# A reordered ramp with dummy matmuls, a last batch gated by token tiles, and out chunks in column tiles: an attention and gated-MLP kernel on one core

## Chip, cores, metric

One core of one Trainium2 chip. The metric is the device time of one execution in microseconds (us), lower is better. An execution takes about 1.8 us more (1.7 to 3.0 in single runs) than its span in the trace, from the first to the last instruction. A run is called fast unless it is over 1.5% above the fastest of the same kernel on that occasion. One of the findings below is that the kernel before has two groups of runs *within* the fast ones, so the text says each time which group it compares.

## The reference

Eight batches. Each is a grouped-query attention (16 query heads, 4 key/value heads, 384 tokens, head size 64), followed by a gated MLP whose gate mixes tokens.

```python
scores = scale * np.matmul(q, k.transpose(0, 1, 3, 2))     # k, v repeated for 4 query heads
attn = np.exp(scores - max); attn = attn / (sum + 1e-09)
x = concat_heads(np.matmul(attn, v))                       # (8, 384, 1024)
h = np.maximum(x @ w_in, 0.0)                              # (8, 384, 1024)
u, v = h[..., :512], h[..., 512:]
v_n = (v - mean(v)) / np.sqrt(var(v) + 1e-06)
v_s = np.einsum('ts,bsd->btd', w_spatial, v_n) + b_spatial[None, :, None]
return ((u * v_s) @ w_out).astype(np.float32)              # (8, 384, 1024)
```

## The kernel before

The whole program is a text of steps, played in order. Each word names a function: `s` a pair of score matmuls, `e` their exp on ScalarE (ACT), `a` an add of two exp tiles on VectorE (DVE), `m` the row sums, `r` the reciprocal, `x` the value matmuls, `n` the normalisation to xT, `V` and `U` the two halves of the w_in product, `S` the statistics, `rs` the rstd, `vn` v_n, `p` the spatial product, `O` an out chunk of 512 columns, `l..` loads, `c..` casts to half precision, `K`, `Q`, `t..` transposes, `A`, `H` half products of V and U. A quote mark means the batch before, a plus the batch after. So a steady round works on three batches at once.

```python
def play(b, text):
    for word in text.split():
        ...                       # letters: the step; digits: its arguments; ' and +: the batch
            STEPS[op](at, *nums)

def pe_group(dst, pairs):
    n = len(pairs)
    for i, (w, m) in enumerate(pairs):
        nc.tensor.matmul(dst, w, m, start=(i == 0), stop=(i == n - 1))

def project(b, i, split=1):       # O: gT (128x128 weights) times w_out16, 4 matmuls of 512 columns
    ...
    pe_group(banks[:, x, :], [(gT[:, m, tt*P:(tt+1)*P], w_out16[:, m, half*512:(half+1)*512]) for m in range(NDT)])
    nc.vector.tensor_copy(osb[:, half * 512 : (half + 1) * 512], banks[:, x, :])
    ...                           # split == 2: a write of 256 KB for each half

RAMP = "lkg0 lqd00 lqd01 lv lkg1 lqd10 lqd11"
RAMP1 = """
    ckv0 cqv000 cqp001 Ka0 Qj00 Qja01 wv0 cqv010 cqv011
    s0 e0 s1 e1 s2 e2 Q01 ckv1 cqv100 cqv101 s3 e3 K1 s4 e4 Q10 cqv110 cqv111 s5 e5 Q11
    cv wu0 lk+ lq0+ lq1+ lv+ ws ck+ cq0+ wv1
    s6 e6 s7 m00 r00 x000 n000 x001 n001 e7 s8 e8 s9 e9 s10
    ...
    m11 r11 x110 n110 x111 n111 Q10+ Q11+ cws tws"""
C1 = "m10' m11' r10' r11' x100' n100' x101' n101' x110' n110' x111' n111'"
C0 = "m00 m01 r00 r01 x000 n000 x001 n001 x010 n010 x011 n011"
VISITS = [
    "s0 s1 s2 e0 e1 e2 a12' O0'' O1'' lk+ lq0+ lv+ lq1+", C1,
    "s3 s4 s5 e3 e4 e5 V0' S0' V1' S1' a00 a01 ck+ cq0+",
    "s6 s7 s8 e6 e7 e8 V2' S2' O2'' O3'' tk+ tq0+ cq1+ cv+",
    "s9 s10 s11 e9 e10 e11 a02 O4'' rs' O5'' vn' tq1+", C0,
    "s12 s13 s14 e12 e13 e14 p0' U0' p1' U1' a10",
    "s15 s16 s17 e15 e16 e17 p2' U2' p3' U3' a11",
]
...
LAST = """
    a12' O0'' O1'' m10' m11' r10' r11' x100' n100' x101' n101' x110' n110' x111' n111'
    V0' S0' V1' S1' O2'' V2' S2' O3'' rs' vn' O4'' O5''
    p0' p1' U0' p2' U1' p3' U2' U3' O0' O1' O2' O3' Oh4' Oh5'"""

play(0, RAMP); ...; play(0, RAMP1); play(1, FIRST)
for b in range(2, B):
    play(b, STEADY if b > 2 else ...)
play(B, LAST)
```

The softmax here doesn't subtract the row's maximum and nothing guards it: scores larger than these inputs give would overflow.

Of the kernel before, what the change touches and what calls it, by code (L numbers as in the profile page):

```python
# [10 lines left out]
FP32 = mybir.dt.float32  # L11
FP16 = mybir.dt.float16
# [5 lines left out]
def kernel(  # L18
# [11 lines left out]
    nc = tc.nc  # L30
# [53 lines left out]
    def touch(*xs):  # L84
        mark(False, xs)

    def take1():
        x = min((i for i in range(8) if not busy[i]), key=lambda i: used[i])
        mark(True, (x,))
        return x  # L90

    def take2():
# [4 lines left out]
        mark(True, (x, x + 1))  # L97
        return x, x + 1

    def f32(x, n):  # L100
        return banks[:, x, 0:n]

    def f16(x, n):
        return banks[:, x, :].bitcast(FP16)[:, 0:n]

    def pe_group(dst, pairs):
        n = len(pairs)
        for i, (w, m) in enumerate(pairs):
            nc.tensor.matmul(dst, w, m, start=(i == 0), stop=(i == n - 1))  # L109


    ident = cst.tile([P, P], FP32, name="ident")
    ident16 = cst.tile([P, P], FP16, name="ident16")
    ones32 = cst.tile([P, 32], FP16, name="ones32")
    eps_t = cst.tile([P, 1], FP32, name="eps_t")
    bias_raw = cst.tile([P, S], FP32, name="bias_raw")
# [69 lines left out]
    def cast_v(b, engine):  # L186
        engine(T["v16", b].rearrange("p g t d -> p g (t d)"), T["v32", b])

    def load_q(b, gp, qds=(0, 1)):
        if ("q32", b, gp) not in T:  # L190
            T["q32", b, gp] = ld.tile([P, 2, G, NST * D], FP32, name=f"q32_{b}_{gp}", tag=f"q32_{gp}")
            T["q16", b, gp] = qk16.tile([P, G, NST, 2, D], FP16, name=f"q16_{b}_{gp}", tag=f"q16_{gp}")
        heads = q[b, gp * 2 * G : (gp + 1) * 2 * G].rearrange(
            "(a qd) (p t) d -> qd p a (t d)", qd=2, t=NST
        )
        for qd in qds:
            nc.sync.dma_start(T["q32", b, gp][:, qd, :, :], heads[qd])

    def cast_q(b, gp, engine, half, qd):
        engine(  # L200
            T["q16", b, gp][:, 2 * qd : 2 * qd + 2, :, half, :],
            T["q32", b, gp][:, qd, 2 * half : 2 * half + 2, :].rearrange(
                "p j (t d) -> p j t d", t=NST
            ),
        )
# [36 lines left out]
    def turn_q_pe(b, gp, js, copy):  # L242
# [14 lines left out]
        )  # L257
        touch(x)


    def score(b, u):
        gp, c, t = u // 9, (u % 9) // 3, u % 3
# [36 lines left out]
    def add(b, gp, c):  # L299
# [3 lines left out]
        cs = slice(c * 512, (c + 1) * 512)  # L303
        nc.vector.tensor_tensor(T["sT", b, gp][:, :, cs], aT[:, 0, :, cs], aT[:, 1, :, cs], ALU.add)  # L304

    def sums(b, gp, quad):
        x = take1()
        aT, sT = T["aT", b, gp], T.get(("sT", b, gp))
        parts = [aT[:, t] for t in range(NST)] if sT is None else [sT, aT[:, 2]]
        tiles(f32(x, S), quad, [(ones32, a) for a in parts])  # L310
        T["sum", b, gp, quad] = x

    def recip(b, gp, quad):
# [4 lines left out]
        nc.scalar.activation(rec, rec, AF.Exp, scale=-1.0)  # L318
        T["rec", b, gp, quad] = rec

    def value(b, gp, quad, jj):
        v16, aT = T["v16", b], T["aT", b, gp]
        x = take1()
        tiles(
            f32(x, S),
            quad,
            [
                (v16[:, 2 * gp : 2 * gp + 2, t, 32 * jj : 32 * (jj + 1)], aT[:, t])
                for t in range(NST)
            ],  # L330
        )
        T["X", b, gp, quad, jj] = x
# [24 lines left out]
        )  # L357
        return x

    def v_half(b, st):  # L360
        x = v_mm(b, st, range(4))
        if ("vparts", b) not in T:
            T["vparts", b] = ff.tile([P, NST, DH], FP32, name=f"vparts_{b}", tag="part")
        part = T["vparts", b][:, st, :]
        nc.vector.tensor_copy(part, banks[:, x, :])
        touch(x)
        T["vpart", b, st] = part

    def u_half(b, mu):
        x = u_mm(b, mu, range(4))  # L370
        if ("uparts", b) not in T:
            T["uparts", b] = ff.tile([P, NDT, S], FP32, name=f"uparts_{b}", tag="part")
        part = T["uparts", b][:, mu, :]
        nc.vector.tensor_copy(part, f32(x, S))
        touch(x)
        T["upart", b, mu] = part

# [64 lines left out]
        )  # L442
        touch(x)

    def project(b, i, split=1):
        tt, half = i // 2, i % 2
        if half == 0:
            T["osb", b, tt] = outp.tile([P, DM], FP32, name=f"osb_{b}_{tt}", tag="osb")
        osb = T["osb", b, tt]
        gT = T["gT", b]  # L450
        x = take1()
        pe_group(
            banks[:, x, :],
            [
                (gT[:, m, tt * P : (tt + 1) * P], w_out16[:, m, half * 512 : (half + 1) * 512])
                for m in range(NDT)
            ],
        )
        nc.vector.tensor_copy(osb[:, half * 512 : (half + 1) * 512], banks[:, x, :])  # L459
        touch(x)  # L460
        dst = out[b].rearrange("(p t) d -> p t d", t=NST)[:, tt, :]
        if split == 2:
            nc.sync.dma_start(
                dst[:, half * 512 : (half + 1) * 512], osb[:, half * 512 : (half + 1) * 512]
            )
        elif half == 1:
            nc.sync.dma_start(dst, osb)

    vec, act, pool = nc.vector.tensor_copy, nc.scalar.copy, nc.gpsimd.tensor_copy




    STEPS = {
        "s": score, "e": expo, "m": sums, "a": add, "r": recip, "x": value, "n": norm,
        "V": gate_v, "S": stats, "rs": rstd, "vn": lambda b: v_norm(b, nc.vector),
        "p": spatial, "U": gate_u, "O": project, "A": v_half, "H": u_half,
        "lk": load_k, "lq": load_q, "lv": load_v,
        "lkg": lambda b, gp: load_k(b, (gp,)),
        "lqd": lambda b, gp, qd: load_q(b, gp, (qd,)),  # L480
        "ck": lambda b: cast_k(b, pool), "cv": lambda b: cast_v(b, pool),
        "ckv": lambda b, gp: cast_k(b, vec, (gp,)),
        "cq": lambda b, gp: [cast_q(b, gp, pool, half, qd) for qd in range(2) for half in range(2)],
# [4 lines left out]
        "K": lambda b, gp: turn_k_pe(b, gp, vec),  # L488
        "Ka": lambda b, gp: turn_k_pe(b, gp, act),
        "Q": lambda b, gp, i: turn_q_pe(b, gp, (2 * i, 2 * i + 1), vec),  # L490
        "Qj": lambda b, gp, j: turn_q_pe(b, gp, (j,), vec),
        "Qja": lambda b, gp, j: turn_q_pe(b, gp, (j,), act),
        "wv": lambda b, gp: load_w_in(gp, DH, DFF), "wu": lambda b, gp: load_w_in(gp, 0, DH),
        "wo": lambda b: load_w_out(), "ws": lambda b: load_ws(),
        "cws": lambda b: cast_ws(nc.gpsimd), "tws": lambda b: turn_ws(),
        "Oh": lambda b, i: project(b, i, 2),
    }

    def play(b, text):
        for word in text.split():  # L500
            kind = word.rstrip("'+")
            at = b - word.count("'") + word.count("+")
            op = kind.rstrip("0123456789")
            nums = kind[len(op):]
            if 0 <= at < B:
                STEPS[op](at, *([int(nums)] if op in ("s", "e") else map(int, nums)))

    RAMP = """
        lkg0 lqd00 lqd01 lv lkg1 lqd10 lqd11"""
    RAMP1 = """  # L510
        ckv0 cqv000 cqp001 Ka0 Qj00 Qja01 wv0 cqv010 cqv011
        s0 e0 s1 e1 s2 e2 Q01 ckv1 cqv100 cqv101 s3 e3 K1 s4 e4 Q10 cqv110 cqv111 s5 e5 Q11
        cv wu0 lk+ lq0+ lq1+ lv+ ws ck+ cq0+ wv1
        s6 e6 s7 m00 r00 x000 n000 x001 n001 e7 s8 e8 s9 e9 s10
        m01 r01 x010 n010 x011 n011 e10 A0 s11 e11 A1 s12 e12 A2 s13 e13 H0 s14 e14
        K0+ K1+ s15 e15 Q00+ m10 r10 x100 n100 x101 n101 cq1+ wu1 cv+ wo
        s16 e16 Q01+ s17 e17 H1 s0+ e0+ H2 s1+ e1+ H3 s2+ e2+
        m11 r11 x110 n110 x111 n111 Q10+ Q11+ cws tws"""
    C1 = "m10' m11' r10' r11' x100' n100' x101' n101' x110' n110' x111' n111'"
    C0 = "m00 m01 r00 r01 x000 n000 x001 n001 x010 n010 x011 n011"  # L520
    VISITS = [
        "s0 s1 s2 e0 e1 e2 a12' O0'' O1'' lk+ lq0+ lv+ lq1+", C1,
        "s3 s4 s5 e3 e4 e5 V0' S0' V1' S1' a00 a01 ck+ cq0+",
        "s6 s7 s8 e6 e7 e8 V2' S2' O2'' O3'' tk+ tq0+ cq1+ cv+",
        "s9 s10 s11 e9 e10 e11 a02 O4'' rs' O5'' vn' tq1+", C0,
        "s12 s13 s14 e12 e13 e14 p0' U0' p1' U1' a10",
        "s15 s16 s17 e15 e16 e17 p2' U2' p3' U3' a11",
    ]
    STEADY = " ".join(VISITS)
    FIRST = " ".join(w for w in STEADY.replace(C1, "").split() if w not in ("s0", "s1", "s2", "e0", "e1", "e2", "a12'", "a00", "a01", "a02", "a10", "a11"))  # L530
    LAST = """
        a12' O0'' O1'' m10' m11' r10' r11' x100' n100' x101' n101' x110' n110' x111' n111'
        V0' S0' V1' S1' O2'' V2' S2' O3'' rs' vn' O4'' O5''
        p0' p1' U0' p2' U1' p3' U2' U3' O0' O1' O2' O3' Oh4' Oh5'"""

    with tc.manual_schedule():
        play(0, RAMP)
        make_identity(nc, ident)
        nc.vector.tensor_copy(ident16, ident)
        nc.vector.memset(ones32, 1.0)  # L540
        nc.vector.memset(eps_t, eps_ln)
        play(0, RAMP1)
        play(1, FIRST)
        for b in range(2, B):
            play(b, STEADY if b > 2 else " ".join(w for w in STEADY.split() if w != "a12'"))
        play(B, LAST)
# [1 line left out]
_INS = ['q', 'k', 'v', 'moe_w_in', 'moe_w_spatial', 'moe_b_spatial', 'moe_w_out']  # L548
# [26 lines left out]
```

## Time and profile before

| kernel before | |
|---|---|
| time, median of 3 runs | 263.55 us (262.69 to 263.74) |
| span of the profiled run | 260.4 us (that run took 262.19) |
| TensorE (PE) busy | 242.8 us, 93% of the span |
| DVE, ACT, Pool busy | 186.5, 172.6, 58.4 us |
| second value steps of batch 1 begin | 58.89 us |
| last batch's second value steps begin | 232.00 us |

The last two rows cut the span in three: a ramp (58.89 us), a steady middle of twelve half rounds (173.11 us) and a tail (28.42 us). "Value steps" are always the 48 matmuls aT,v of 384 columns, which PE does in one go twice in a batch (the steps C0 and C1 of the text). They are a mark that a trace of either kernel has. Where only a batch is named below, its second ones, C1, are meant. Note that the profiled run took 262.19 us and the three timed ones 262.69 to 263.74: the trace shows one of the quicker runs. That will matter.

### The profile page before, as it was taken

The page shows a single profiled execution, that of the slowest core. Times are in us where ns is not written, and L with a number is a line of the kernel's source. Part 1 is how long each engine was busy: PE and PEld are TensorE (multiplying, and loading weights), DVE is VectorE, ACT ScalarE, POOL GpSimd, SP SyncE. Part 2 cuts the span into 40 slices and gives each one's busy share as a digit, 9 for nine tenths or more (in the row PEclk, how much of TensorE's full clock was granted, in tenths as well). Part 3 has the DMA queues.
Part 4 walks back from the last instruction along what each step waited for, and adds up shares of the span by engine and source line. Part 5 has one row for each costly group of instructions (what it writes and reads, how often), then busy time and mean ns, then how long its engine had stood idle before and what let it go on. Part 6 is the DMA issues. An engine that isn't in the chain of part 4 may idle for free.

```text
span 260.4 us, 5301 instructions
## 1 busy us (share of the span) xinstructions
PE 242.8 (93%) x2140; PEld 110.8 (43%) x2140; DVE 186.5 (72%) x345; ACT 172.6 (66%) x227; POOL 58.4 (22%) x100
## 2 busy tenths in 40 slices
PE   2798998799999999999999999999899999999993
PEld 1333443344355444444354434543354434554451
DVE  2434658885986779766986689676986689587954
ACT  2877989787685877676785868776775858730000
POOL 3639704400720045001800054002600000000000
PEclk9999999999999999999999999999999999999999
DMA  7999999807694299609692398709592204010306
GB/s 213 258 302 303 171 197 317 136 0 242 205 211 104 92 303 184 182 4 277 190 241 51 117 326 136 181 27 280 174 237 45 83 0 164 0 64 20 161 1 242
DMA packets 56920, 41.92 MB, mean 161 GB/s; under 512 B 26304, under 2 KB 53056, under 8 KB 56896
## 3 DMA queue, kind: packets, MB, share of 16 engines
q1 hardware_dynamic: 54048, 38.44, 54.7%
q0 software_dynamic: 2848, 3.15, 7.4%
q8 instruction: 16, 0.26, 0.4%
q14 instruction: 8, 0.07, 0.1%
HBM read 25.95 MB, written 12.58 MB: 148 GB/s over the span
## 4 chain that ended last, share of the span: by engine, by line
PE 67%; DVE 18%; DMA 4%; ACT 4%; issue 3%; SPq 2%; POOL 0%; DVEq 0%
PE banks L109 46%; PE banks L269 10%; PE banks L291 9%; DMA q<-in_q_dram 4%; DVE xT L338 4%; DVE v_n L407 3%; DVE osb L459 3%; ACT aT L281 3%; PE banks L250 2%; DVE sT L304 2%; DVE bn L396 1%; DVE v_r L383 1%; DVE vs L427 1%; DVE uparts L438 1%; SPq L170 1%
## 5 line engine op out<-in xcount | busy, mean ns | idle before, releaser
L281 ACT ACTIVATE aT<-banks 128x1024 f16<-128x1024 f32 x144 | 137.7, 1024 | 50.1 <-PE banks L269 50.0
L269 PE MATMUL banks<-qT,kT 64*128 64x512 f16 x288 | 46.7, 393 | 5.7 <-DVE osb L459 2.0
L109 PE MATMUL banks<-xT,w_in 128*128 128x384 f16 x256 | 47.4, 326 | 0.0
L109 PE MATMUL banks<-w_out,gT 128*128 128x512 f16 x192 | 45.7, 380 | 0.1
L109 PE MATMUL banks<-w_in,xT 128*128 128x512 f16 x192 | 45.1, 380 | 0.7 <-DVE xT L338 0.6
L338 DVE TENSOR_TENSOR xT<-banks,rec 128x384 f16<-128x384 f32 x64 | 31.4, 549 | 14.3 <-ACT rec L318 12.3
L200 POOL CAST q<-q 128x384 f16<-128x384 f32 x57 | 31.8, 587 | 16.3 <-DMA q<-in_q_dram 12.7
L459 DVE COPY osb<-banks 128x512 f32<-128x512 f32 x48 | 32.1, 685 | 4.5 <-PE banks L109 4.2
L291 PE MATMUL banks<-aT,v 128*32 128x384 f16 x768 | 35.3, 332 | 0.0
L109 PEld LDWEIGHTS <-w_in 128*128 128x128 f16 x256 | 24.7, 98 | 17.0 <-issue 0.9
L176 POOL CAST k<-k 128x768 f16<-128x768 f32 x7 | 5.8, 830 | 111.6 <-DMA k<-in_k_dram 111.6
L109 PEld LDWEIGHTS <-gT 128*128 128x128 f16 x192 | 17.5, 98 | 29.8 <-issue 9.3
L440 DVE SCALAR_TENSOR_TENSOR gT<-banks,vs 128x384 f16<-128x384 f32 x28 | 15.6, 557 | 19.3 <-PE banks L109 19.2
L109 PEld LDWEIGHTS <-xT 128*128 128x128 f16 x192 | 17.4, 98 | 26.5 <-issue 6.8
L304 DVE TENSOR_TENSOR sT<-aT 128x1024 f16<-128x1024 f16 x36 | 26.6, 765 | 0.0
L291 PEld LDWEIGHTS <-v 128*32 128x32 f16 x768 | 21.1, 99 | 11.0 <-issue 0.9
L383 DVE TENSOR_SCALAR v_r<-banks 128x512 f32<-128x512 f32 x21 | 14.4, 688 | 12.9 <-PE banks L109 12.3
L269 PEld LDWEIGHTS <-kT 64*128 64x128 f16 x288 | 10.9, 95 | 28.9 <-issue 23.1
L109 PE MATMUL banks<-wsT,v_n 128*128 128x384 f16 x96 | 21.1, 326 | 1.1 <-DVE v_n L407 0.3
L427 DVE TENSOR_TENSOR vs<-banks,bias_tp 128x384 f32<-128x384 f32 x32 | 17.7, 556 | 3.1 <-PE banks L109 3.1
L316 ACT ACTIVATE rec<-banks 128x384 f32<-128x384 f32 x32 | 15.5, 485 | 5.7 <-PE banks L291 5.5
L318 ACT ACTIVATE rec<-rec 128x384 f32<-128x384 f32 x32 | 16.7, 523 | 1.0
(40 smaller groups left out, 130.2 us busy)
## 6 DMA issues: line engine op xcount, KB each, us to landing
q<-in_q_dram SPq DMA_DIRECT2D x32, 384.0 KB, 6.8
out_dram<-osb SPq DMA_DIRECT2D x23, 512.0 KB, 3.4
v<-in_v_dram SPq DMA_DIRECT2D x8, 384.0 KB, 6.3
k<-in_k_dram SPq DMA_DIRECT2D x7, 384.0 KB, 5.4
w_in<-in_moe_w_in_dram POOLq DMA_DIRECT2D x16, 128.0 KB, 5.7
w_out<-in_moe_w_out_dram POOLq DMA_DIRECT2D x2, 512.0 KB, 7.2
ws<-in_moe_w_spatial_dram SPq DMA_DIRECT2D x1, 576.0 KB, 9.3
out_dram<-osb SPq DMA_DIRECT2D x2, 256.0 KB, 2.4
```

What stands on the lines that cost most here:

```text
L109: nc.tensor.matmul(dst, w, m, start=(i == 0), stop=(i == n - 1))
L200: engine(T["q16", b, gp][:, 2 * qd : 2 * qd + 2, :, half, :], T["q32", b, gp][:, qd, 2 * half : 2 * half + 2, :].rearrange("p j (t d) -> p ...
L269: nc.tensor.matmul(banks[:, xs[half], :], T["kT", b][lo:hi, t, gp, :], rhs[lo:hi, c * 512 : (c + 1) * 512], start=True, stop=True,)
L281: nc.scalar.activation(T["aT", b, gp][:, t, :, c * 512 : (c + 1) * 512], banks[:, x : y + 1 : y - x, :], AF.Exp, scale=scale)
L291: nc.tensor.matmul(dst[32 * i : 32 * (i + 1), :], weights if len(weights.shape) == 2 else weights[:, half, :], a[:, half, j * S : (j + 1) ...
L304: nc.vector.tensor_tensor(T["sT", b, gp][:, :, cs], aT[:, 0, :, cs], aT[:, 1, :, cs], ALU.add)
L318: nc.scalar.activation(rec, rec, AF.Exp, scale=-1.0)
L338: nc.vector.tensor_tensor(T["xT", b][:, gp * 4 + quad * 2 + jj, :], f32(x, S), T["rec", b, gp, quad], ALU.mult)
L383: nc.vector.tensor_scalar(v_r, banks[:, x, :], 0.0, None, op0=ALU.max)
L427: nc.vector.tensor_tensor(vs, f32(x, S), bias_tp, ALU.add)
L440: nc.vector.scalar_tensor_tensor(T["gT", b][:, mu, :], src, 0.0, T["vs", b, mu], op0=ALU.max, op1=ALU.mult)
L459: nc.vector.tensor_copy(osb[:, half * 512 : (half + 1) * 512], banks[:, x, :])
```

## The change

Its intent: start the exp stream sooner (q by quad index in 192 KB pieces, dummy matmuls that bring TensorE to full clock before there is data), rebuild the order of the first two batches, save changes of tile form beside the 32-column steps, and shorten the last batch's serial end.

```diff
-    def pe_group(dst, pairs):
+    def pe_group(dst, pairs, cols=P):
         n = len(pairs)
         for i, (w, m) in enumerate(pairs):
-            nc.tensor.matmul(dst, w, m, start=(i == 0), stop=(i == n - 1))
+            for c in range(0, P, cols):
+                nc.tensor.matmul(dst[c : c + cols], w[:, c : c + cols], m, start=(i == 0), stop=(i == n - 1))
+    def idle(b, n):                            # step w: n dummy matmuls, 128 columns
+        x = take1()
+        for _ in range(n):
+            nc.tensor.matmul(f32(x, P), warm, warm, start=True, stop=True)
+        touch(x)
+    def load_qj(b, gp, j): ...                 # step lqj: q of one quad index, 192 KB
     def sums(b, gp, quad):
-        x = take1()
+        x = take_of_pair(("sums", b, gp)) if b else take1()   # value steps: likewise, pairs of banks
+    def spatial_all(b, m): ...                 # pz: as p, but keeps all four vs chunks
+    def gate_u_tile(b, tt):                    # Uz: u product and gate of one 128-token tile
+        for mu in range(NDT):
+            pe_group(banks[:, x, mu*P:(mu+1)*P], [(w_in16[:, kc, mu*P:(mu+1)*P], T["xT", b][:, kc, ts]) for kc in range(NKT)])
+        nc.vector.scalar_tensor_tensor(T["gT", b][:, :, ts], ...)
+    def project_last(b, i, parts=2):           # Oz: two 256-column halves, copied by DVE and ACT,
+        ...                                    #     written from two queues, 128 KB each
+        "Oc": lambda b, i: project(b, i, cols=32),
     RAMP = """
-        lkg0 lqd00 lqd01 lv lkg1 lqd10 lqd11"""
+        lqj00 lkg0 lqj01 lqd01 lkg1 lqd10 lv lqd11"""
     RAMP1 = """
-        ckv0 cqv000 cqp001 Ka0 Qj00 Qja01 wv0 cqv010 cqv011
-        s0 e0 s1 e1 s2 e2 Q01 ckv1 ... s3 e3 K1 s4 e4 Q10 cqv110 cqv111 s5 e5 Q11
+        w23 cqjv00 Qja00 w6 ckv0 cqjp01 Ka0 w2 Qj01 wv0 cqv010 cqv011
+        w2 s0 e0 s1 e1 s2 e2 Q01 ckv1 ... s3 e3 s4 e4 K1 s5 e5 Q10 cqv110 cqv111 s6 e6 s7 e7
         ...
-        m11 r11 x110 n110 x111 n111 Q10+ Q11+ cws tws"""
+        H1 s1+ e1+ m11 r11 s2+ e2+ x110 n110 x111 n111 Q10+ tws"""
-        "s0 s1 s2 e0 e1 e2 a12' O0'' O1'' lk+ lq0+ lv+ lq1+", C1,
+        "s0 s1 s2 e0 e1 e2 a12' Oc0'' Oc1'' lk+ lq0+ lv+ lq1+", C1,
-        "s9 s10 s11 e9 e10 e11 a02 O4'' rs' O5'' vn' tq1+", C0,
+        "s9 s10 s11 e9 rs' e10 e11 a02 Oc4'' Oc5'' vn' tq1+", C0,
-    FIRST = (STEADY without C1, the first three scores and the adds)
+    FIRST = """lk+ lq0+ lv+ lq1+
+        s3 e3 s4 e4 V0' S0' s5 e5 V1' S1' ck+ cq0+
+        s6 e6 s7 e7 V2' S2' s8 e8 Q11 tk+ tq0+ cq1+ cv+
+        s9 e9 s10 e10 rs' tq1+ H2' H3' m00 m01 r00 r01 s11 e11 vn' x000 ... n011
+        s12 e12 s13 e13 p0' U0' s14 e14 p1' U1'
+        s15 s16 s17 e15 e16 e17 p2' U2' p3' U3' a10 a11"""
     LAST = """
-        a12' O0'' O1'' ...
-        V0' S0' V1' S1' O2'' V2' S2' O3'' rs' vn' O4'' O5''
-        p0' p1' U0' p2' U1' p3' U2' U3' O0' O1' O2' O3' Oh4' Oh5'"""
+        a12' Oc0'' Oc1'' ...
+        V0' S0' V1' S1' V2' S2' O2'' O3'' rs' vn' O4'' O5''
+        pz0' pz1' pz2' pz3' Uz0' Uz1' O0' O1' Uz2' Oh2' Oh3' Oh4' Oz5'"""
```

Some steps of the full diff are defined and never played (a reciprocal on DVE, a third add, copies on ACT). They play no part.

## The prediction

> **What bounds the kernel now.** I read the views in this order: the page's chain, stretches of the span, the timeline of each end, then the timeline of TensorE (PE) alone for one batch. The chain first:
>
> ```profile
> PE 67%; DVE 18%; DMA 4%; ACT 4%; issue 3%; SPq 2%; POOL 0%; DVEq 0%
> ```
>
> TensorE owns two thirds of the path, but not everywhere. The stretches (length, then busy us of PE, PEld, DVE, ACT, POOL, each with its count) show where:
>
> ```profile
> 36.00:56.00 20.00, 17.34 (x157) 7.65 (x155) 17.69 (x34) 16.86 (x23) 5.83 (x10) 1.00 0.87 179
> 85.40:114.07 28.67, 28.58 (x257) 13.08 (x258) 21.84 (x41) 21.14 (x29) 6.26 (x10) 1.00 0.65 173
> 230.20:260.40 30.20, 25.69 (x177) 12.28 (x177) 21.06 (x38) 2.42 (x6) 0.00 (x0) 1.00 0.26 105
> ```
>
> One steady batch takes 28.67 us and PE is busy all of it. The ramp up to 56 us is different: PE, DVE and ACT share it, none is full, and waits pass between them. The last 30 us are PE again, with a tail of 4 us. In the ramp's timeline (start, length, engine, line, what, idle before):
>
> ```profile
> 8.44 0.82 PE L250 MATMUL banks<-ident,q 128*128 128x128 f16 x6
> 14.91 1.02 ACT L281 ACTIVATE aT<-banks 128x1024 f16<-128x1024 f32 x1 [1.05 <-PE banks L269]
> 23.35 1.02 ACT L281 ACTIVATE aT<-banks 128x1024 f16<-128x1024 f32 x1 [0.95 <-PE banks L269]
> 27.67 0.51 PE L250 MATMUL banks<-ident,q 128*128 128x128 f16 x6
> ```
>
> The same six transposes take 0.82 us at 8.4 us and 0.51 us at 27.7 us: PE is on half clock at first. A score pair shows it too (0.61 us at 12.18, 0.39 us at 22.92). From the first exp (7.69) to the last of batch 1 (58.30) ACT has 50.6 us, of which its idle entries add up to 6.8 us. The chain in order of time then shows what ends the ramp:
>
> ```profile
> 39.90 5.61 ACT aT L281 x6
> ...
> 47.36 0.72 DVE v_n L407
> 48.08 1.40 DVE xT L338 x3
> 49.52 0.66 PE banks L109 x3
> ...
> 56.11 0.57 DVE gT L440
> 56.72 1.25 PE banks L109 x5
> ```
>
> Batch 0's gate: six exps in ACT's queue ahead of rstd, then v_n, the norms of batch 1, and a DVE chain of vs, uparts and gT, 1.6 us for each of four chunks, until 56.68. In the steady state, PE alone:
>
> ```profile
> 71.03 1.90 PE L109 MATMUL banks<-w_out,gT 128*128 128x512 f16 x8
> 72.86 0.35 PE L291 MATMUL banks<-sT,ones 128*32 128x384 f16 x4
> ...
> 90.63 3.63 PE L109 MATMUL banks<-w_in,xT 128*128 128x512 f16 x16
> 94.19 0.82 PE L269 MATMUL banks<-qT,kT 64*128 64x512 f16 x6
> 94.94 1.90 PE L109 MATMUL banks<-w_in,xT 128*128 128x512 f16 x8
> 96.68 1.89 PE L109 MATMUL banks<-w_out,gT 128*128 128x512 f16 x8
> ```
>
> From 94.94 to 96.68 no tile form changes: eight 512-column matmuls in 1.74 us, 0.217 each. From 71.03 to 72.86 the same eight are followed by a change from the whole array to 32-column tiles: 1.83, so the change costs 0.10 us. Sixteen at 90.63 end in a change to scores: 3.56 against 16 x 0.216 = 3.45, again 0.10. A batch makes 14 such changes, 1.4 us.
>
> **What the Trainium skill says.** "TensorEngine Tiling (Array Packing)", section Tiling Modes, Key Properties: "Changing tiling mode (not just tile) drains the TensorE". The trace agrees, 0.10 us a change. The same page, Restrictions and Gotchas, says that column tiling excludes Fast Weight Load; but in this trace four 32-column value matmuls of 384 columns pass in 0.162 us with their four weight loads, the pace of one whole-array matmul of that length, so I see no price. "TensorE: Matmul & The Clock Gate", Part 1, says that the array starts at half clock and is let to full clock after about 3.4 us of sustained work. The 0.82 against 0.51 us agrees in kind; when the change comes in this trace (between the slow pair at 12.18 and the fast one at 22.92) depends on how densely PE works.
>
> **Part 1, the ramp.** It loads q by quad, 192 KB pieces: q(j=0), k, q(j=1) instead of k and two 384 KB pieces. Before, k was usable at 3.43 and q at 4.88, so 384 KB took 1.45 us. In the new order q(0) comes near 3.4, k near 4.2, q(1) near 4.9. Pool's cast of q(1) takes 0.7 (to 5.6), transpose 0.5, copy 0.36: first scores near 6.5 instead of 7.05. The dummies (31 in all) run before that, in time that PE was idle; they cost nothing unless the last ones hold up a transpose, 0.2 us. With full clock from about 7 us the first exp comes 0.43 us after its scores instead of 0.64: near 7.1, a gain of 0.6.
>
> Then ACT's own work: 36 exps at 0.98, six reciprocals at 1.0, one rstd 0.5: 42 us. Following the new order on PE, ACT and DVE with the durations above, I find no ACT wait up to exp 17 of batch 0 (two scores now lie ahead of each exp, and Q10/Q11 and the half products A0 to A2 no longer stand between them); one wait of 1.0 us where batch 1's K and Q copies gather on DVE (before, they were spread); V0 of batch 0 at 33.2 instead of 37.65; rstd after exp 10 instead of 11, near 41 instead of 45.3; v_n from 42.2 instead of 45.95, then four norms to 46, and the DVE chain of 6.4 us to 52.5 instead of 56.68. Here it gives some back: the three adds of batch 1 now stand on DVE between gT and the sums (two 0.7 us adds before the first sum can run), so the value steps come near 55.1 instead of 58.89. That is 3.8 us by a tally that knows no bad luck; I take 3.5.
>
> **Part 2, out chunks in column tiles.** It makes 4 matmuls and 4 loads of each, with no more streaming, and removes two changes a batch. Beside the C1 steps the 0.10 us counts. Beside C0 the step behind is p0, which waits for DVE norms (0.24 us idle around 105), and these follow the copy of the last out chunk: there most is lost. So 0.1 to 0.2 a batch, times six: 0.9 us. The bank order in the steady batch comes out the same step for step, rstd moved up one place is still followed by v_n behind the out copies on DVE, so I count nothing for those.
>
> **Part 3, the last batch.** The end before:
>
> ```profile
> 250.90 5.52 PE L109 MATMUL banks<-w_out,gT 128*128 128x512 f16 x24
> 251.72 4.21 PEld L109 LDWEIGHTS <-gT 128*128 128x128 f16 x21 [0.50 <-DVE gT L440]
> 256.46 0.69 DVE L459 COPY osb<-banks 128x512 f32<-128x512 f32 x1 [0.17 <-PE banks L109]
> ```
>
> The 0.50 us wait for the last gT goes, as token tile 0's gate is done while tile 1 is multiplied. The u product becomes 96 matmuls of 128 columns instead of 32 of 384: at 0.056 us (twelve transposes start within 0.84 us) 5.4 against 5.2. V2 before the old out chunks changes little, since DVE reaches v_n at 242.5 either way: two out copies stand ahead of it. The last 512 columns go as two halves, copied by DVE and ACT and sent on two queues: copy about 0.4 instead of 0.69, and a 128 KB write about 0.3 shorter than a 256 KB one (median 2.4, an estimate). Sum: 0.5 - 0.2 + 0.6 = 0.9 us.
>
> **Sum.** 3.5 + 0.9 + 0.9 = 5.3 us, 258.2. My tally leaves out the changes of tile form saved where the new ramp runs two scores together, and the waits for osb copies in batches 1 and 2 (0.3 us each); 0.4 us for those gives 257.8.
>
> **Rivals.** (a) The ramp's waits only move: DVE is already 17.7 of 20 us busy between 36 and 56, the new order puts H2, H3, a Q11 copy and the adds on it there, and batch 2's q arrives by DMA (share 0.87 there) as late as before. Then the ramp gives 1.5 and the total is about 260. For it: v_n took 2.1 us there instead of 1.46. Against: rstd in before stood behind ACT and DVE both. (b) The dummies don't bring full clock, or it is lost again as PE waits: then the first 10 us keep their slow transposes, 1 us less gain, 259. Against it: before, it came by itself with far less work. (c) Column tiles with the whole 128-row weights of gT don't keep the pace, say 0.3 instead of 0.217 a group: 16 groups a batch, 1.3 us each, 9 us in all, and the time is unchanged or worse. Against it: the value matmuls keep theirs at 20 ns an instruction, and 512 columns ask only 27. (d) The ramp is better than tallied and the whole batch gains 0.3 from the changes: 255.
>
> **Range and chances.** The ramp is the wide term, 1.5 to 5; the others 0.3 to 1.8 and 0.3 to 1.5. Combined, 255.0 to 260.6. Two per cent is at 258.3, just above my middle, so faster is only a little likelier than same; slower would need rival (c).
>
> **What would show it.** Right: six transposes near 0.5 us by 10 us; first exp near 7.1; gT of batch 0 complete near 52.5; value steps of batch 1 near 55; steady batches of 28.4 to 28.6 with no 0.10 us between out chunks and sums; no weight wait for gT in the last batch. Wrong: out groups longer than 0.22 us in column tiles, batch 1's scores waiting for K and Q copies by over 1.5 us, or gT later than 54.5.

## The result, and the profile after

The changed kernel takes 256.89 us (median of 4 runs, 256.78 to 257.06), the kernel before in the same series 263.64 (262.69 to 264.58). The ratio is 0.9745, 95% interval 0.9709 to 0.978: faster. A ratio here and below is the mean time of one kernel's fast runs over that of the other's of the same rounds, so it is not quite the ratio of the medians.

The marks in the two traces:

| | before | after | difference |
|---|---|---|---|
| ramp, to batch 1's value steps | 58.89 | 55.55 | -3.34 |
| twelve half rounds | 173.11 | 171.57 | -1.54 |
| tail | 28.42 | 28.08 | -0.34 |
| span | 260.4 | 255.2 | -5.2 |

The traces differ by 5.2 us, the medians by 6.75. The missing 1.5 us is no instruction of either trace; the first experiment suggests where it comes from.

The page first: the chain that ended last by engine, and the row of the granted clock in 40 slices.

```profile
PE 57%; DVE 19%; DMA 12%; POOL 5%; SPq 3%; issue 3%; ACT 0%
PEclk9589999999999999999999999999999999999998
```

Transfers hold 12% of the path where they held 4%, and ACT's 4% are gone from it. The clock is full in the first slice, half in the second: the dummies brought it, and it was lost again, which the following rows of the ramp's timeline date. (The row says nothing of the time before the clock record's first entry, 4.18 us here: before has a 9 in all its slices, its first entry is at 18.07, and its first transposes take 0.82 us.)

```profile
5.96 0.50 POOL L226 CAST q<-q 128x384 f16<-128x384 f32 x1 [4.66 <-DMA q<-in_q_dram]
7.74 7.55 ACT L321 ACTIVATE aT<-banks 128x1024 f16<-128x1024 f32 x8 [2.39 <-PE banks L309]
8.47 0.82 PE L282 MATMUL banks<-ident,q 128*128 128x128 f16 x6
11.89 0.82 PE L282 MATMUL banks<-ident,q 128*128 128x128 f16 x6
15.79 0.51 PE L282 MATMUL banks<-ident,q 128*128 128x128 f16 x6
```

Six transposes cost 0.82 us at 8.47 and 11.89 and 0.51 only at 15.79. The clock record agrees: full from 4.18 to 7.6, half to 14.42, full for the rest. The second quad of q landed at 5.96, where the prediction had 4.9, and the first exp began at 7.74, where before had 7.69. But from there eight exps run without a gap, in 7.55 us, where the first eight of before took 10.70. Up to rstd, the step that releases batch 0's gate, ACT has these two rows, before and after (columns as in the prediction, then granted clock, DMA share, GB/s):

```profile
7.69:45.34 37.65, 34.62 (x345) 14.73 (x345) 20.73 (x42) 32.65 (x38) 19.70 (x35) 1.00 1.13 257
7.74:40.97 33.23, 30.74 (x295) 12.61 (x295) 19.18 (x41) 30.93 (x37) 17.67 (x31) 0.90 1.14 223
```

From the first exp to rstd it took 37.65 us before and 33.23 after: ACT has 30.93 us of work there instead of 32.65 (29 exps ahead of rstd instead of 30), and 2.3 us without work instead of 5.0.

The end of the ramp, on DVE:

```profile
42.16 2.01 DVE L460 TENSOR_SCALAR v_n<-v_r,mv,rstd 128x512 f16<-128x512 f32 x3
...
52.24 0.58 DVE L493 SCALAR_TENSOR_TENSOR gT<-uparts,vs 128x384 f16<-128x384 f32 x1
52.75 1.88 DVE L344 TENSOR_TENSOR sT<-aT 128x1024 f16<-128x1024 f16 x3
```

rstd came on ACT at 40.97 (before 45.3), v_n at 42.16 (45.95), the last gT complete at 52.82 (56.68). The chain of waits in order of time, though, arrives at the same place by another road:

```profile
38.12 8.62 DMA q<-in_q_dram
...
46.79 1.30 POOL q L232 x2
48.10 4.18 DMA qT<-q
...
52.41 0.82 PE banks L309 x6
```

Batch 2's q: 8.62 us from issue to landing, two casts on Pool, a transposing DMA, then batch 2's first scores. On PE:

```profile
52.41 0.82 PE L309 MATMUL banks<-qT,kT 64*128 64x512 f16 x6 [1.47 <-DMA qT<-q]
53.17 1.91 PE L119 MATMUL banks<-w_out,gT 128*32 128x512 f16 x32
54.91 0.34 PE L331 MATMUL banks<-sT,ones 128*32 128x384 f16 x4
...
55.55 2.12 PE L331 MATMUL banks<-aT,v 128*32 128x384 f16 x48
```

There is a new wait of 1.47 us before the scores, and the gate (52.82) and q (52.28) are now ready within about half a microsecond of each other. The second and third rows are the column tiles: 32 matmuls of 512 columns, four at a time, last 1.74 us to the sums (53.17 to 54.91). That is eight groups at 0.217 with nothing left for a change of form; before it was 1.83.

The tail, on PE and then at the very end on all engines:

```profile
237.91 2.71 PE L119 MATMUL banks<-wsT,v_n 128*128 128x384 f16 x12
240.45 3.74 PE L119 MATMUL banks<-xT,w_in 128*128 128x128 f16 x64
...
247.54 3.63 PE L119 MATMUL banks<-w_out,gT 128*128 128x512 f16 x20
```

```profile
251.20 0.37 ACT L571 COPY osb<-banks 128x256 f32<-128x256 f32 x1 [14.43 <-PE banks L119]
251.47 0.41 SPq L572 DMA_DIRECT2D out_dram<-osb  x1
251.60 0.37 ACTq L572 DMA_DIRECT2D out_dram<-osb  x1
```

From the first spatial matmul to the end of the last out matmul: 237.91 to 251.17, 13.26 us; before 243.16 to 256.42, 13.26 us. The gating by token tiles moved nothing there. From the end of the last copy to the end of the span: 251.57 to 255.2, 3.63 us, before 3.25 (257.15 to 260.4).

### The profile page after: what moved, and what is told of

Same layout as the page of the kernel before. It is cut to its first block, busy times and chain, and to the rows that moved or that the text cites. A ratio compares the mean times of both kernels' runs of the same rounds, so it can differ in the third digit from the quotient of the medians.

```text
span 255.2 us, 6119 instructions
## 1 busy us (share of the span) xinstructions
PE 242.1 (95%) x2545; PEld 117.2 (46%) x2545; DVE 186.5 (73%) x348; ACT 172.1 (67%) x228; POOL 57.9 (23%) x100
## 4 chain that ended last, share of the span: by engine, by line
PE 57%; DVE 19%; DMA 12%; POOL 5%; SPq 3%; issue 3%; ACT 0%
PE banks L119 43%; DMA q<-in_q_dram 8%; PE banks L331 7%; PE banks L309 7%; DVE osb L513 4%; DVE sT L344 3%; DVE bn L449 3%; DVE v_n L460 3%; DVE v_r L436 3%; DVE xT L391 3%; DMA v<-in_v_dram 2%; POOL w_in L142 2%; DMA qT<-q 2%; POOL q L232 2%; SPq L210 1%
## 5 line engine op out<-in xcount | busy, mean ns | idle before, releaser
L119 PE MATMUL banks<-xT,w_in 128*128 128x384 f16 (+1 forms) x320 | 47.2, 294 | 0.6 <-DVE v_r L438 0.6
L119 PE MATMUL banks<-w_out,gT 128*32 128x512 f16 (+2 forms) x508 | 45.4, 378 | 0.0
L119 PEld LDWEIGHTS <-w_in 128*128 128x128 f16 x320 | 27.3, 98 | 15.8 <-issue 1.4
L331 PE MATMUL banks<-aT,v 128*32 128x384 f16 x768 | 34.4, 326 | 0.0
L513 DVE COPY osb<-banks 128x512 f32<-128x512 f32 x47 | 31.2, 684 | 3.5 <-PE banks L119 3.4
L119 PEld LDWEIGHTS <-gT 128*32 128x32 f16 (+1 forms) x508 | 18.8, 96 | 27.1 <-issue 8.8
L344 DVE TENSOR_TENSOR sT<-aT 128x1024 f16<-128x1024 f16 x39 | 27.7, 738 | 0.0
L493 DVE SCALAR_TENSOR_TENSOR gT<-banks,vs 128x384 f16<-128x384 f32 x24 | 13.4, 558 | 17.0 <-PE banks L119 17.0
L331 PEld LDWEIGHTS <-v 128*32 128x32 f16 x768 | 20.3, 97 | 11.1 <-issue 0.8
L480 DVE TENSOR_TENSOR vs<-banks,bias_tp 128x384 f32<-128x384 f32 x28 | 15.6, 556 | 2.8 <-PE banks L119 2.8
```

Source lines behind the costliest of these rows:

```text
L119: nc.tensor.matmul(dst[c : c + cols], w[:, c : c + cols], m, start=(i == 0), stop=(i == n - 1))
L331: nc.tensor.matmul(dst[32 * i : 32 * (i + 1), :], weights if len(weights.shape) == 2 else weights[:, half, :], a[:, half, j * S : (j + 1) ...
L344: nc.vector.tensor_tensor(T["sT", b, gp][:, :, cs], aT[:, 0, :, cs], aT[:, 1, :, cs], ALU.add)
L480: nc.vector.tensor_tensor(vs, f32(x, S), bias_tp, ALU.add)
```

## The experiments

Twelve kernels ran, four in each of three series, each series on one chip with its own runs of the kernel before. All gave correct results. The edits are against the changed kernel unless said.

| kernel | median us (range, runs) | before in its series | ratio, 95% |
|---|---|---|---|
| a_old_ramp | 261.44 (258.94-263.35, 20) | 262.60 | 0.9917 (0.9885-0.9949) |
| a_no_cols | 257.04 (256.51-257.64, 4) | 262.60 | 0.9762 (0.9703-0.9821) |
| a_old_last | 256.70 (256.32-258.37, 4) | 262.60 | 0.9768 (0.9709-0.9827) |
| a_no_dummies | 257.38 (256.46-259.79, 4) | 262.60 | 0.9796 (0.9726-0.9865) |
| b_early_loads | 261.09 (258.04-263.84, 20) | 263.28 | 0.9918 (0.9881-0.9955) |
| b_early_bridge | 259.43 (258.11-261.74, 20) | 263.28 | 0.9899 (0.9866-0.9932) |
| b_early_no_dummies | 261.57 (259.60-265.13, 12) | 263.28 | 0.9968 (0.9930-1.0006) |
| b_v2_first | 256.85 (256.56-257.00, 4) | 263.28 | 0.9822 (0.9767-0.9877) |
| c_after (unaltered) | 257.45 (256.50-260.27, 6) | 262.53 | 0.9801 (0.9757-0.9846) |
| c_before_fill | 262.38 (260.94-265.51, 22) | 262.53 | 0.9995 (0.9971-1.0019) |
| c_early_kq0 | 257.16 (256.51-257.56, 6) | 262.53 | 0.9774 (0.9742-0.9805) |
| c_halves | 257.39 (256.76-257.93, 6) | 262.53 | 0.9789 (0.9759-0.9819) |

The unaltered kernel lies at 256.89 in one series and 257.45 in another. So medians of four to six runs that differ by less than some 0.6 us are not told apart here.

### a_old_ramp: the ramp of before, all else of after

```diff
-    lqj00 lkg0 lqj01 lqd01 ...  w23 cqjv00 Qja00 w6 ...   (RAMP, RAMP1, FIRST of after)
+    lkg0 lqd00 lqd01 lv ...     ckv0 cqv000 cqp001 ...    (RAMP, RAMP1, FIRST of before)
-        x, pairs[key] = take2(); return x
+        return take1()
```

The last two lines take back the allotment of banks in pairs as well, in all batches.

> The ramp and batch 1's first round put back as before (loads, order, no dummies, no bank pairs, three-part sums); column tiles and the new last batch kept. Theory (the ramp gave 3.3 us, from 58.89 to 55.55 at the value steps of batch 1, as the two profiles show): the time rises by 3.3 to 4, to 260.2 to 260.9. Rival (the profile of before was a lucky run and part of the gain is that steady batches no longer lose time at random, which came with the ramp's phase of DMA and Pool work): the rise is 4.5 or more and single steady batches of 29 us and above come back.

Measured: 261.44 us, 4.5 us more than after. But the 20 runs are two groups, told apart by the mean granted clock of the run. Ten with a clock of 0.997 or more average 259.60 us. Eight with 0.993 or less average 262.40 (the six of these that count as fast: 262.13). A mean of 0.993 is what one half-clock stretch of 3.4 us makes of a 260 us span (0.5 x 3.4 / 260 = 0.0066). The profiled run is of the second group. PE in it, around 50 us:

```profile
48.79 0.84 PE L306 MATMUL banks<-qT,kT 64*128 64x512 f16 x2 [0.84 <-DVE xT L388]
...
50.33 1.49 PE L116 MATMUL banks<-xT,w_in 128*128 128x384 f16 x4
```

and in the trace of before, a run of the first group:

```profile
50.01 0.81 PE L109 MATMUL banks<-xT,w_in 128*128 128x384 f16 x4
```

The same four matmuls last 1.49 instead of 0.81 us. The windows from 48 to 52 us (columns: length; busy us of PE, PEld, DVE, ACT, Pool with counts; granted clock; DMA share; GB/s) of a_old_ramp,

```profile
48.00:52.00 4.00, 3.03 (x11) 1.33 (x11) 2.83 (x7) 2.80 (x4) 1.40 (x2) 0.76 0.82 165
```

have a clock of 0.76 where before has 1.00, and 11 matmuls where before has 18. The clock record shows half clock for 3.413 us from 50.05 us. It falls after a stretch (46.8 to 49.7) in which PE stood in waits of 0.71 and 0.84 us for ACT and DVE and worked little between (1.18 of 2.9 us). But the trace of before has waits of 0.56 and 0.92 us in the same place, 1.32 us of work in the same stretch, and keeps the clock. So the stretch alone does not decide; what does, no run shows.

With this in hand I sorted all runs of before over the three series: 96 runs (one of 405 us left out). 50 have a clock of 0.997 or more and average 261.90 us; 40 have 0.993 or less and average 264.29; 6 lie between. Among runs that count as fast alone the two are 261.90 (50) and 263.92 (27), so this is no mere slow state. The kernel before loses some 2 to 2.4 us in about two runs of five. The first two timed series (263.55, 263.64) lie nearer to that group by their times; no clock was read for them.

So the ramp is worth 2.3 to 2.7 us between undisturbed runs (259.60 less 257.26 and 256.91, the means of the changed kernel in two other series), and as much again in each run in which the old ramp loses the clock. Column tiles and tail together come to 261.96 - 259.60 = 2.4 us, with the undisturbed runs of before in this series. The profiled run of a_old_ramp has a tail that is 0.36 us shorter than that of after (27.72 against 28.08), for a reason that has nothing to do with the ramp (see "Last batch" below). If all its runs have it, the ramp is worth 0.4 us more and the other two 0.4 us less. Even then 2.0 us for column tiles and tail is more than the traces show for them (0.9 and 0.3), and taking away one alone costs nothing that the runs show (next two sections). Where the rest lies is open.

### a_no_cols: out chunks on the whole array

```diff
-        "Oc": lambda b, i: project(b, i, cols=32),
+        "Oc": lambda b, i: project(b, i),
```

> The changed kernel with the four out chunks beside the value steps on the whole array again. Theory (one change of tile form of 0.10 us less per C1, and nothing beside C0): rises by 0.6 to 0.9 us, the gap from the out chunks to the sums goes back to 1.83 us. Rival (both sides count): 1.3 us. Rival (column tiles are slower or equal): no change or faster.

Measured: 257.04 us, not to be told from after. The trace, on PE:

```profile
95.92 1.90 PE L119 MATMUL banks<-w_out,gT 128*128 128x512 f16 x8
97.75 0.35 PE L331 MATMUL banks<-sT,ones 128*32 128x384 f16 x4
```

The 0.09 to 0.10 us is back (1.83 to the sums). The twelve half rounds take 172.98 us. Over all traces, the eleven with column tiles give 171.57 to 172.76 (mean 172.18), and the three without 173.11, 172.98 and 173.07 (mean 173.05): 0.9 us. In the steady rounds the gap from the out chunks to the sums is 1.74 us with column tiles and 1.83 without, beside C0 as well as C1. Beside C0 the gain is lost again behind them: from the value steps to the first spatial matmul, which waits for a norm on DVE, it takes 3.08 to 3.10 us in after and 2.95 to 3.06 in before. From there to C1 0.11 is left (11.24 against 11.35). a_no_cols has 2.95 to 2.96 and 11.35. The rest of the 0.9 us lies between C1 and C0, where single half rounds scatter (14.2 to 14.8 us with, 14.3 to 15.3 without). Shown in the traces, then, and too small for the timed runs.

### a_old_last and b_v2_first: the tail

```diff
# a_old_last
-        V0' S0' V1' S1' V2' S2' O2'' O3'' rs' vn' O4'' O5''
-        pz0' pz1' pz2' pz3' Uz0' Uz1' O0' O1' Uz2' Oh2' Oh3' Oh4' Oz5'"""
+        V0' S0' V1' S1' O2'' V2' S2' O3'' rs' vn' O4'' O5''
+        p0' p1' U0' p2' U1' p3' U2' U3' O0' O1' O2' O3' Oh4' Oh5'"""
# b_v2_first: V2 before the out chunks stays, the gate and the last chunk of before
-        pz0' pz1' pz2' pz3' Uz0' Uz1' O0' O1' Uz2' Oh2' Oh3' Oh4' Oz5'"""
+        p0' p1' U0' p2' U1' p3' U2' U3' O0' O1' O2' O3' Oh4' Oh5'"""
```

> The changed kernel with the old order of the last batch (old gate by chunk, V2 after an out chunk, one last write of 256 KB). The prediction's size: rises by 0.9 us. What the two profiles show (from the last value steps to the end 28.42 before, 28.08 after): rises by 0.3 to 0.4 us.

> The changed kernel with the old gate by chunks and one last write, but V2 before the old out chunks as in the change. From the two profiles: V2 first brought v_n 0.37 us earlier (8.13 against 8.49 us after V0's start), and gating by token tiles and the split write brought nothing (13.26 us from the first spatial matmul to the last matmul in both; 3.6 against 3.3 us from the last copy to the end): within 0.15 us of the changed kernel. The prediction's sizes: 0.9 us slower.

Measured: 256.70 and 256.85 us, the same as after within the noise. The traces are sharper. The tail from the last value steps is 28.36 us in a_old_last, 27.99 in b_v2_first, 28.08 in after and 28.42 in before. In both kernels that do V2 first, the spatial product begins 8.73 us after V0 (before 9.10): that is 0.37 us, as much as the tail gained in all. b_v2_first needs 13.27 us from the first spatial matmul to the last out matmul (238.02 to 251.29), like after and before.

### a_no_dummies: without the 33 dummy matmuls

```diff
-        w23 cqjv00 Qja00 w6 ckv0 cqjp01 Ka0 w2 Qj01 wv0 cqv010 cqv011
-        w2 s0 e0 s1 e1 ...
+        cqjv00 Qja00 ckv0 cqjp01 Ka0 Qj01 wv0 cqv010 cqv011
+        s0 e0 s1 e1 ...
```

> The changed kernel without the 33 dummy matmuls. The prediction's idea: up to 1 us slower, as the clock comes late. Theory after the result: the full clock the dummies bring is lost while TensorE waits 1.6 us for q of quad 1 (transposes at 8.5 us take 0.82 us again), and the start of batch 2 waits for its q by DMA at 52.4 us whatever the first 15 us do: no change, within 0.2 us.

Measured: 257.38 us; three runs without a clock drop average 257.08, one with a drop took 259.79. In the trace full clock comes at 15.97 us, the first exp at 7.82, the value steps at 55.22 (after: 55.55). The first timed runs of after say the same in another way: two with a mean clock of 0.983 and 0.984, which is a half-clock stretch of the length seen early in its trace, took 256.98 and 256.78 us, and two with 0.998 took 256.81 and 257.06. Seven microseconds of half clock at the start cost nothing that shows: the first eight exps take 7.56 us in this trace and 7.44 in b_v2_first, which has full clock from 4.69 us. Nor do the dummies bring the clock each time. Of the traces with the same 33, three have it from 4.5 to 5.1 us on and keep it past 48 us (a_old_last, b_v2_first, b_early_loads), after loses it again, c_halves gets it at 9.5 us, and a_no_cols, c_after and c_early_kq0 at 12.9 to 13.7, about when b_early_no_dummies has it without any (12.94).

### b_early_loads, b_early_bridge, b_early_no_dummies: batch 2's loads earlier

The 1.47 us wait for batch 2's q suggested that its loads should be issued before the transpose of the spatial weights (`tws`).

```diff
-        H1 s1+ e1+ m11 r11 s2+ e2+ x110 n110 x111 n111 Q10+ tws"""
+        H1 s1+ e1+ m11 r11 s2+ e2+ x110 n110 x111 n111 Q10+ lk++ lq0++ lv++ lq1++ tws"""
-    FIRST = """lk+ lq0+ lv+ lq1+
+    FIRST = """
```

b_early_bridge has 24 dummies in place of `w2` before `Qj01` as well, to keep the clock until the scores. b_early_no_dummies has no dummies.

> The changed kernel with batch 2's loads issued before the transpose of the spatial weights, which on the sync queue waits for Pool until 33 us and holds them back to 35.3 us. Theory (batch 2 starts at 52.41 because its q, cast and transposed by DMA, comes then): the 1.47 us wait before batch 2's first scores goes, value steps of batch 1 start near 54.9 instead of 55.55 or earlier, as the gate's DVE chain (52.82) is then next; 0.6 to 1.1 us faster. Rival (the DVE chain and the adds behind it set the end of the ramp anyway): under 0.3 us.

> Early loads, and 24 dummies instead of 2 while TensorE waits for q of quad 1. Theory that the ramp is ACT and DVE work: the full clock is kept from some 5 us on (six transposes near 8.5 us take 0.5 instead of 0.82 us), exps and gate come 0.3 to 0.8 us earlier than with early loads alone, and so does the end. Rival: the clock hardly matters, within 0.2 us.

> Early loads and no dummies at all. If the dummies were useless only because batch 2's q came late, this one loses 0.3 us or more against early loads alone; if the clock hardly matters it is within 0.2 us of it.

Measured: 261.09, 259.43 and 261.57 us, 2.5 to 4.7 us slower than after. The theory fell. b_early_loads, on the load queue and on PE:

```profile
36.24 5.83 SPq L171 DMA_TRANSPOSE wsT<-ws  x1
```

```profile
47.61 0.65 PE L119 MATMUL banks<-wsT,v_n 128*128 128x384 f16 x3 [3.25 <-DMA wsT<-ws]
```

and the transpose in after:

```profile
33.07 2.18 SPq L171 DMA_TRANSPOSE wsT<-ws  x1
```

The DMA engines are full from 18 to 36 us (share 1.11 in after, 1.14 here), so loads issued earlier only push back what stood behind them. The spatial-weight transpose is issued 3.2 us later, takes 5.83 instead of 2.18 us to issue, and the gate of batch 0 waits 3.25 us for it.

These three kernels also show the clock again. After the 3.25 us wait the clock is half from 48.9 to 52.3 us, in a place where the trace of after does not have it. The share of runs with 0.993 or less goes with the length of that wait in the profiled run: 14 of 20 with 3.25 us, 10 of 12 with 3.32 us, 4 of 20 with 1.63 us (bridge). This mark also counts runs that lost the clock early, as after did (0.983), so the shares are no clean count of this drop. In b_early_bridge the clock was full from 6.7 us to the end, and the runs with 0.997 or more average 259.18 against 259.52 in b_early_loads. That pair does not price the early clock: the trace of b_early_loads kept it as well (from 4.5 us), the wait differs, and the 24 dummies held up the transposes (q cast at 5.77 and transposed at 7.14, against 5.80 and 6.36 in b_v2_first), so that the first exp came at 8.35.

### c_early_kq0: only k and the first half of q earlier

```diff
-        ... Q10+ tws"""
+        ... Q10+ lk++ lq0++ tws"""
-    FIRST = """lk+ lq0+ lv+ lq1+
+    FIRST = """lv+ lq1+
```

> The changed kernel with only k and the first half of q of batch 2 loaded ahead of the spatial weights' transpose (loading all four ahead made that transpose 5 us late and the kernel 4 us slower). Theory (the start of batch 2 waits for k and q, 0.3 to 1.5 us in five of six profiles): that wait goes and the spatial transpose stays at 33 us, 0.3 to 1 us faster. Rival (DMA is full between 18 and 36 us, so whatever goes first makes something else late): within 0.3 us, or slower, with another wait on a DMA in its place.

Measured: 257.16 us beside 257.45 for the unaltered kernel of the same series: no gain. In its trace the transpose of the spatial weights again takes 5.88 us to issue. PE:

```profile
51.65 0.82 PE L309 MATMUL banks<-qT,kT 64*128 64x512 f16 x6 [0.43 <-DMA qT<-q]
```

A wait of 0.43 us is left, but the unaltered kernel's own trace in this series has 0.49. The 1.47 us was the worst of the traces, not the rule (0.31 to 0.81 in four others with the same loads, none in a_no_cols). No gain from the order of these loads shows.

### c_halves: q by the old halves, order otherwise new

```diff
-        lqj00 lkg0 lqj01 lqd01 lkg1 lqd10 lv lqd11"""
+        lkg0 lqd00 lqd01 lkg1 lqd10 lv lqd11"""        (RAMP1 as in after)
```

> The changed kernel with the first loads as in before (k, then q in 384 KB halves) instead of by quad. The prediction's idea (192 KB pieces bring the first scores earlier): first exp later, about 7.4 or more, and the kernel up to 0.5 us slower. Rival (q of quad 1 lands between 5.0 and 6.0 us in ten profiles, not at 4.9, since the pieces share the engines with what is issued behind them; the halves landed at 4.9): first exp at 7.0 to 7.3, no slower.

Measured: 257.39 us, as c_after. The first exp comes at 8.32 us, 0.3 to 1.2 later than in the seven other kernels that have the new ramp without the four early loads (7.16 to 8.01), and the value steps at 55.61, the latest of the eight. The equal time does not show that the start is harmless, for this kernel too has the end that is 0.4 us shorter (tail 27.70 against 28.06 to 28.11 in the others with the new last batch). The traces say the opposite: in all eleven with the new ramp rstd comes 33.1 to 33.3 us after the first exp, and in the eight just named the value steps come 47.0 to 47.8 after it. So a later first exp is passed on, to rstd in full and to the value steps for the most part. By this reading q by halves cost some 0.4 us here; no run alters the start alone with the end kept equal.

### c_after and c_before_fill: is the clock the missing 1.5 us?

c_after is the changed kernel again. c_before_fill is the kernel *before* with nine dummy matmuls on PE ahead of batch 1's score 13, in the stretch after which the clock falls:

```diff
+    def fill(b, n):
+        x = T["sum", b, 0, 0]
+        for _ in range(n):
+            nc.tensor.matmul(banks[:, x, 0:P], ident16, ident16, start=True, stop=True)
-    FIRST = " ".join(...)
+    FIRST = " ".join(...).replace("s13", "w9 s13")
```

> The changed kernel unaltered, as the reference of this series on the same chip: 256.6 to 257.1 us, nearly all runs with a mean clock of 0.997 or more (or 0.983 where the early full clock is lost), none with the half-clock stretch at 50 us.

> The kernel before, with 9 dummy matmuls put in the 0.56 us in which TensorE waits for a reciprocal ahead of score 13 of batch 1 (about 46.7 us). Theory (half of the runs of before lose the full clock for 3.4 us near 50 us, as TensorE does too little in the window before it, and these runs are the ones at 263.4 to 264.7 us with a mean clock of 0.991 to 0.993, against 260.6 to 262.3 us at 0.999 to 1.0): the slow runs become rare, the median falls from 263 to 261.5 to 262. Rival (the clock record only goes along with something else that makes these runs late): the same two groups in the same shares, median unchanged or up.

Measured: c_after 257.45 us, with one run of six at a clock of 0.993 and 260.27 us, so the new order is not wholly free of it. c_before_fill 262.38 us, no faster than before (262.53). Of its 22 runs 3 have a clock of 0.993 or less (mean 264.59), of the 27 of before in this series 8 (264.26). Undisturbed runs average 262.21 against 262.13. So drops were rarer, but 3 of 22 against 8 of 27 is a weak difference, and the median did not come down as the clock theory asked. Its profiled run fell in the disturbed group, half clock from 50.23 us, with the fill in place. That the runs with a drop are 2 to 2.5 us longer, and that the same matmuls take nearly twice as long in it, the traces show. That waits on PE bring the drop is supported by b_early_loads, where making a wait brought it in the profiled run. This experiment does not support it: filling a part of the stretch did not reliably take it away.

No kernel among the twelve beats the changed one by more than its own spread.

## Why the prediction was right, and where it was wrong

The prediction was 257.8 us (255.0 to 260.6), faster only a little likelier than same. Measured: 256.89, faster. By its own steps:

**Ramp, 3.5 us: right in size, and right in its main mechanism.** Between the traces 3.34. The chain that was tallied came out closely: rstd near 41 (40.97), v_n from 42.2 (42.16), last gT near 52.5 (52.82), value steps near 55.1 (55.55). a_old_ramp confirms it with 2.3 to 2.7 us between undisturbed runs (0.4 more, if the shorter end of that kernel is counted). It took back the allotment of banks in pairs too, so the two are not told apart.

**First exp at 7.1 us by the quads and the dummies: wrong, and made good by a second error.** q's second quad landed at 5.96 and not 4.9, the clock fell back to half from 7.6 to 14.42 (rival b), and the first exp began at 7.74, no earlier than before. The step's own estimate of 0.6 us for it was not earned. The tally then took 33.9 us from the first exp to rstd (7.1 to 41), and the trace has 33.23. The two errors, 0.6 and 0.7 us, cancel, and that is why every later mark came out so closely: in part luck. The gain of the ramp is in what lies between first exp and rstd, 33.23 us instead of 37.65, and not in its start, which came no sooner than before. Rival (b) happened in this trace, and its price of 1 us was wrong. Two slips of the prediction changed nothing: the dummies are 33 and not 31, and the exps up to 58.30 are 39, three of them of batch 2 (the last of batch 1 ends at 55.18).

**Rival (a), batch 2's q late: happened in part.** The wait of 1.47 us for it is new. The prediction gave this road 260 us if it ruled; it only became level with the gate. Seven other traces with the new ramp end it at 54.18 to 55.61, 2.2 us after the last gT (after: 2.7), so in those the gate rules and not q.

**Column tiles, 0.9 us: right.** The pace of 0.217 us a group was kept, ruling out rival (c). The 0.10 us beside C1 went, and beside C0 it was lost, as argued. 0.9 us between traces with and without. (Steady batches take 28.65 to 28.79 us where the prediction had 28.4 to 28.6; before 28.67 to 29.59.) The 0.4 us added for other waits makes 1.3 against a measured middle of 1.54. Of the two extras named, the wait for an osb copy is still there (0.28 us before score 11 of batch 3).

**Last batch, 0.9 us: wrong, 0.34.** The term "- 0.2" for short matmuls was right (96 at 0.056 are 5.38 us, 32 of 384 columns are 5.2), and the others failed, each its own way.

- The 0.50 us wait for gT went, as predicted, but it was a wait of PE's weight load, beside matmuls that were still running. PE's own loss is the row of 24 out matmuls, 5.52 us, less 24 x 0.216 and 0.17 for the last one's drain (16 of them last 3.63 where 16 x 0.216 is 3.46): 0.17 us. The gate by token tiles saved that and paid as much in short matmuls. From the first spatial matmul on it comes to nothing (13.26 us in both).
- The copy did shrink: it ends 0.40 us after the last matmul instead of 0.73, 0.3 as predicted.
- The shorter write, which the prediction put at 0.3 without saying from what, brought nothing. From the end of the last copy to the last landing it is 2.28 us in both traces (251.57 to 253.85, 257.16 to 259.44): the last 128 KB piece, on ACT's queue, lands 2.25 us after its issue, the last 256 KB piece of before 2.26. "DMA: Bandwidth & Descriptors", section Anatomy of one DMA, of the Trainium skill gives a DMA a fixed cost of about 2.0 us besides its bytes (a fit over DMAs issued from GpSimd, which these are not), and these landings are of that size.
- The end gave the copy's gain back: 1.35 us from the last landing to the end of the span, before 0.98. The packed traces hold the reason, in records that no view prints. At the end SyncE (SP) waits for the semaphores of the transfers one after the other, in steps of 0.06 us. In after the write that lands last has semaphore 101, and behind that wait seven further ones stand; in before one stands there. After is one of eight traces with two queues and seven further waits, and they have 1.34 to 1.36 us. The other two with two queues, c_halves and a_old_ramp, where the last write has the last semaphore of the row (118), have 0.97 and 0.99, and tails of 27.70 and 27.72 us. So it is not the second queue. No run moved that semaphore alone.
- "V2 before the old out chunks changes little" was wrong in the other direction: it is the 0.37 us by which v_n came sooner. With 0.3 for the copy, nothing for gate and write, and 0.37 lost at the end, this makes the 0.3 of the tail.

**The base of the sum: a term that was missing.** The differences came from a trace of 262.19 us and were taken off a median of 263.55. By its steps the prediction took off 5.7 us, and the traces differ by 5.2. Taken off the traced run's own 262.19, the measured 5.2 gives 257.0, which is what after takes. The other 1.4 us were in the median already, most likely as runs in which the old ramp lost the clock for 3.4 us. So the predicted total was close because a tail overestimated by 0.6 and a drop that was not foreseen worked against each other.

## What to carry to other kernels

Look at every run's granted clock before explaining a median: a kernel whose engine idles in places can have two groups of runs, and a trace shows one of them. A wait of the weight loads is a loss only as far as the matmuls ahead of it have drained, so read the gap on PE and not on PEld. When a chain of dependencies sets the end of a phase, measure its links from a common mark in every trace: here rstd followed the first exp by the same 33.1 to 33.3 us in eleven kernels, which shows what the order gained and that a late start is passed on, where equal totals had hidden it. Where the DMA engines are full, issuing a load earlier delays another. And look at what follows the last landing: 0.4 us here hung on the order of the last waits.

## What the Trainium skill lacked or had wrong

- "TensorE: Matmul & The Clock Gate", Part 1, What's actually happening: it says that the ramp penalty is under 1% of a typical span and not worth fitting. Here a drop in the middle of the kernel, in 40 of 96 runs of the kernel before, cost 2.0 to 2.4 us each (0.8 to 0.9%). That is within the figure, and yet about a third of the 6.75 us of this change. The length of the stretch, 3.413 us, agrees with its window of 3413 ns.
- The same page has no word on whether full clock is worth buying early with dummies in a kernel. Here full clock came by 5.1 us and stayed past 48 us in three traces with 33 of them, stayed for 3.4 us in one and came at 9.5 to 13.7 us in four, and nothing showed in the time (257.38 without, 256.89 and 257.45 with).
- The same page, Back-to-back issue gap: about 81 ns for a matmul of 128 columns with its weight load in a sustained stream. Here 64 such pairs start within 3.58 us (240.45 to 244.03), 56 ns each.
- No page tells that the order of the last waits counts at the end of a program. Here SyncE waits for the DMA semaphores one by one, 0.06 us each: 1.34 to 1.36 us from the last landing to the end of the span where seven further waits stand behind that of the last write, 0.92 to 0.99 where at most one further wait stands behind it.
- "TensorEngine Tiling (Array Packing)", Key Properties: it gives no size for the drain at a change of mode. Here it is 0.10 us. And four 32-column tiles with their own weight loads keep the pace of the whole array at 512 columns, 0.217 us a group, although the page excludes Fast Weight Load for them.
